# One expert layer in blocks of 512 slots instead of 256, handed to the next layer without a trip through memory

## The chip, the cores and the metric

The kernel runs on one core of a Trainium2 chip. The metric is the device time of one execution in microseconds (us); the median of three runs before the change is 4132.17 us. Engines are named as in the profile: PE (TensorE matmul), PEld (its weight loads), DVE (VectorE), ACT (ScalarE), POOL (GpSimd), SP (SyncE, which here only issues transfers).

## The reference

Three layers follow each other on 8 x 3072 = 24576 tokens of 256 features, all in 32-bit floats.

```
Y = rfft(x, axis=1) * (filt_r + 1j*filt_i);  x = irfft(Y)         # long convolution
e = argmax(x @ w_gate);  g = softmax(x @ w_gate)[e]                # one of 8 experts per token
x = g * (relu(x @ w1[e]) @ w2[e])                                  # 256 -> 1024 -> 256, "routed layer"
h = x @ w_in;  a = 0 if h <= -1, h if h >= 1, else (h+1)**2/4
out = a @ w_out                                                    # 256 -> 2048 -> 256, "dense layer"
```

## The kernel before, in words

**Convolution.** Some 650 us of transforms on all engines. For each of the 8 batches it also computes the gate, and ranks the tokens so that each expert's tokens can be found (`r_gate`, `r_cnt`, `r_rank`, `r_inv`, `r_out`). The ranking of the last two batches runs on while the routed layer has begun.

**Slots.** `slots` deals the tokens out to blocks; each block belongs to one expert. It runs twice: early, with the first 5 batches, for 16 full blocks, and late for the rest. `SURE` blocks are always computed; four more would be computed only if the last of the sure ones did not reach the last token (`rest`). The trace has 792 = 99 x 8 steps of blocks, so exactly the sure 99 ran.

**Routed layer.** A block j has 256 slots and eight steps f. Its tokens are gathered by POOL (`gather`: numbers first, then rows of 256 features), multiplied by the gate (`scale`, DVE), turned by PE (`take`) and split into a high and a low half, because every product is computed as three products of rounded halves. The expert's weights come in four loads of 512 KB (`load_w`, SP), and each step splits a part of them (`split_w`: ACT casts the high half `wh`, DVE or POOL subtracts the low half `wl`). Step f then has six matmuls in `b_in` (into a PSUM tile `h`), a Relu on ACT (`hh`), the low half on DVE (`hl`), and three steps later six matmuls in `b_out` into an accumulator `y1` which lasts for the block's eight steps. At the end of a block DVE copies `y1`, and SP stores it and the token numbers to memory (`s_y1T`, `s_idc`).

**Dense layer.** A chunk c has 512 tokens and sixteen steps. `load_c` reads it back from `s_y1T` and splits it. A step has six matmuls of 512 columns (`c_in`, into `h`), four elementwise instructions (DVE, ACT, DVE, ACT) and a subtraction on POOL, and three steps later twelve matmuls of 256 columns (`c_out`). Its four weight tables are loaded once in 16 transfers of 512 KB (`load_w2`).

**Order.** `run` writes the steps out by hand: first 14 blocks (112 steps, called the lead here), then for each chunk its 16 steps with 16 steps of blocks between them, while blocks last. `play` issues them; `plan` says how many steps ahead of use each load, cast and transpose stands. All engines run their instructions in this written order. The first 40-odd steps are dealt out one for one with the rest of the convolution's program, then two with each piece of the late `slots`; only after that does `dense` open the dense layer's buffers.

**PSUM.** Until `dense`, blocks have two banks for `h`, one tile `xt` for the transposes, one accumulator `y1`; `dense` adds a third `h` and a second `y1`.

Of the kernel before, what the change touches and what calls it, by code (L numbers as in the profile page):

```python
# [26 lines left out]
BLK = 256  # L27
NBLK = 103
EARLY = 5
SURE = 99  # L30
# [3 lines left out]
NE1 = 16  # L34
CH = 512
NCH = NTOK // CH

# [74 lines left out]

def slot_consts():
    c = np.zeros((128, 3 * NBLK + 16), np.float32)
    j = np.arange(NBLK)
    c[:, : 2 * NBLK] = (
        256 * j[None, :, None] + 128 * np.arange(2)[None, None, :] + np.arange(128)[:, None, None]
    ).reshape(128, -1)
    c[:, 2 * NBLK : 3 * NBLK] = j
    c[:8, 3 * NBLK : 3 * NBLK + 8] = np.eye(8)  # L120
    c[:, 3 * NBLK + 8 :] = np.arange(8)
    return c
# [492 lines left out]
def slots(tc, a, st, early, side=None):  # L615
# [4 lines left out]
    nb, j0, j1 = (EARLY, 0, NE1) if early else (NB, NE1, NBLK)  # L620
    J, K = j1 - j0, nb - 1
    per = 512 // J
    with ExitStack() as ctx:
# [4 lines left out]
        cst = p.tile([128, 3 * NBLK + 16], FP32, name="cst")  # L628
        nc.sync.dma_start(cst, a["c_b"])
        iota = cst[:, 0 : 2 * J].rearrange("p (j h) -> p j h", h=2)  # L630
        ij = cst[:, 2 * NBLK : 2 * NBLK + J]
        i8 = cst[:8, 3 * NBLK : 3 * NBLK + 8]
        ce = cst[:, 3 * NBLK + 8 : 3 * NBLK + 16]
# [15 lines left out]
        if early:  # L649
            V.tensor_copy(ti, cum[:, nb, :])  # L650
        else:
            V.tensor_tensor(out=tn, in0=cum[:, nb, :], in1=used, op=ALU.subtract)
            V.tensor_scalar(out=tf, in0=tn, scalar1=float(BLK - 1), scalar2=None, op0=ALU.add)
            V.tensor_copy(ti, tf)
            sums(cb, tn)
        V.tensor_scalar(out=ti, in0=ti, scalar1=8, scalar2=None, op0=ALU.logical_shift_right)
# [7 lines left out]
        V.tensor_scalar(out=Q[:, QO, :], in0=pb[:, 0:8], scalar1=-float(BLK), scalar2=None, op0=ALU.mult)  # L664
        yield
        if early:
            V.tensor_scalar(out=used, in0=pb[:, 0:8], scalar1=-1.0, scalar2=float(NE1), op0=ALU.mult, op1=ALU.add)
            V.scalar_tensor_tensor(out=used, in0=used, scalar=0.0, in1=tf, op0=ALU.max, op1=ALU.min)
            V.tensor_scalar(out=used, in0=used, scalar1=float(BLK), scalar2=None, op0=ALU.mult)
        else:  # L670
            V.tensor_tensor(out=Q[:, QC, :], in0=cb[:, 0:8], in1=Q[:, QO, :], op=ALU.add)
            V.tensor_tensor(out=Q[:, QO, :], in0=Q[:, QO, :], in1=used, op=ALU.add)
# [19 lines left out]
        pp = ctx.enter_context(tc.tile_pool(name="b_ps", bufs=1, space=PSUM, side=side))  # L692
        parts = [(k, min(k + per, NQ)) for k in range(0, NQ, per)]
        ps = []
        for i, (k0, k1) in enumerate(parts):
            ps.append(pp.tile([128, per, J], FP32, name=f"q{i}"))
            nc.tensor.matmul(ps[i][:, : k1 - k0], one[:8], QJ[:, k0:k1], start=True, stop=True)
        C = lambda k: ps[k // per][:, k % per]
        yield
        qs = p.tile([128, NQ, J], FP32, name="qs")  # L700
        for (k0, k1), v in zip(parts, ps):
            nc.scalar.copy(qs[:, k0:k1], v[:, : k1 - k0])
            if not early:
                yield
        ecf = p.tile([1, 2, J], FP32, name="ecf")
        V.tensor_copy(ecf[:, 0], C(QE)[:1])
        V.scalar_tensor_tensor(out=ecf[:, 1], in0=ij[:1], scalar=float(BLK), in1=C(QC)[:1], op0=ALU.mult, op1=ALU.add)
        V.tensor_scalar(
            out=ecf[:, 1], in0=ecf[:, 1], scalar1=float(BLK * j0), scalar2=float(NTOK), op0=ALU.add, op1=ALU.min
# [3 lines left out]
        r = p.tile([128, J, 2], FP32, name="r")  # L713
        x = p.tile([128, J, 2], FP32, name="x")
        KS = K if early else 1
        t = p.tile([128, KS, J, 2], FP32, name="t")
        B = lambda k: qs[:, k].unsqueeze(2).to_broadcast([128, J, 2])
        V.tensor_tensor(out=r, in0=iota, in1=B(QO), op=ALU.add)
        V.tensor_tensor(out=x, in0=r, in1=B(QB), op=ALU.add)
        for k in range(0, K, KS):  # L720
            n = min(KS, K - k)
            tk = t[:, :n]
            over = lambda k: qs[:, k : k + n].unsqueeze(3).to_broadcast([128, n, J, 2])
            V.tensor_tensor(out=tk, in0=r[:].unsqueeze(1).to_broadcast([128, n, J, 2]), in1=over(k), op=ALU.is_ge)
            V.tensor_tensor(out=tk, in0=tk, in1=over(K + k), op=ALU.mult)
            s = tk[:, 0]
            if n > 1:
                s = r
                V.tensor_reduce(out=s, in_=tk.rearrange("p k j h -> p j h k"), op=ALU.add, axis=AX.X)
            V.tensor_tensor(out=x, in0=x, in1=s, op=ALU.add)  # L730
            yield
        V.tensor_scalar(out=st["idx"][:, j0:j1], in0=x, scalar1=float(NTOK - 1), scalar2=None, op0=ALU.min)
# [3 lines left out]
class Ffn:  # L736

    LAG, LEAD, SKIP = 3, 26, (0, 6)  # L740

    def __init__(self, ctx, tc, a, st, nblk=NBLK, nch=NCH):
        self.nc, self.tc, self.a, self.st, self.nblk, self.nch = tc.nc, tc, a, st, nblk, nch
# [10 lines left out]
        self.nh = self.ny = 0  # L754
# [4 lines left out]
        self.E, self.RAW, self.W, self.ROW, self.X, self.H, self.CY, self.ACC, self.OUT = ({} for _ in range(9))  # L759

    def dense(self, ctx):
# [4 lines left out]
        self.gp = pool("c_g", 6)  # L766
        self.cyp, self.ap, self.op = (pool(n, 2, side="right") for n in ("c_cy", "c_a", "c_o"))
        self.ps_h.append(pool("cs_h2", 1, space=PSUM))
        self.ps_y.append(pool("cs_y2", 1, space=PSUM))
# [50 lines left out]
    def gather(self, j, more):  # L820
        nc = self.nc
        on = lambda ap: bass.IndirectOffsetOnAxis(ap=ap, axis=0)
        rows_of = lambda t: t[: S * EARLY] if j < NE1 else t
        if not more:
            ids = self.idp.tile([128, 2, 2], I32, name="ids")
            for h in range(2):
                nc.gpsimd.indirect_dma_start(
                    out=ids[:, h, :], out_offset=None, in_=rows_of(self.a["L"]),
                    in_offset=on(self.st["idx"][:, j, h : h + 1]),
                )  # L830
            self.ROW[j] = [ids]
            return
        ids = self.ROW[j][0]
        for h in range(2):
            r = self.rowp.tile([128, 256], FP32, name="row")
            nc.gpsimd.indirect_dma_start(out=r, out_offset=None, in_=rows_of(self.a["y"]), in_offset=on(ids[:, h, 0:1]))
            self.ROW[j].append(r)

    def scale(self, j):
        ids, *rows = self.ROW[j]  # L840
        for h in range(2):
            self.nc.vector.tensor_scalar(
                out=rows[h], in0=rows[h], scalar1=ids[:, h, 1:2].bitcast(FP32), scalar2=None, op0=ALU.mult
            )

    def take(self, j, i):
        nc = self.nc
        ids, *rows = self.ROW[j]
        ps = self.psx.tile([128, 2, 256], FP32, name="xt")
        for h in range(2):  # L850
            for k in range(2):
                nc.tensor.transpose(ps[:, k, 128 * h : 128 * h + 128], rows[h][:, 128 * k : 128 * k + 128], self.st["ident"])
        hi = self.xp.tile([128, 2, 256], F32R, name="xh")
        lo = self.xp.tile([128, 2, 256], F32R, name="xl")
        self.halves(i, ps[:], hi[:], lo[:], True)
        self.X[j] = (hi, lo)

    def b_in(self, j, f):
        nc = self.nc
        (xh, xl), (wh, wl) = self.X[j], self.W[j, f]  # L860
        o = self.h_tile()[:, :256]
        seq = [(w, x, k) for k in range(2) for w, x in ((wh, xh), (wh, xl), (wl, xh))]
        for n, (w, x, k) in enumerate(seq):
            nc.tensor.matmul(o, w[:, k, :], x[:, k, :], start=n == 0, stop=n == 5)  # L864
        hi = self.hp.tile([128, 256], F32R, name="hh")
        lo = self.hp.tile([128, 256], F32R, name="hl")
        nc.scalar.activation(hi, o, ACTF.Relu)  # L867
        yield
        nc.vector.scalar_tensor_tensor(out=lo, in0=o, scalar=0.0, in1=hi[:].bitcast(FP32), op0=ALU.max, op1=ALU.subtract)  # L869
        self.H[j, f] = (hi, lo)  # L870

    def b_out(self, j, f):
        nc = self.nc
        (hi, lo), (wh, wl) = self.H.pop((j, f)), self.W.pop((j, f))
        if f == 0:
            self.ny = (self.ny + 1) % len(self.ps_y)
            self.ACC["b"] = self.ps_y[self.ny].tile([128, 2, 256], FP32, name="y1")
        acc = self.ACC["b"]
        for d in range(2):
            for n, (w, x) in enumerate(((wh, hi), (wh, lo), (wl, hi))):  # L880
# [291 lines left out]
```

## Time and profile before

| | |
|---|---|
| median of 3 runs (range) | 4132.17 us (4128.89 to 4134.86) |
| the profiled execution | 4136.24 us, of which span of the profile 4134.3 us |
| PE busy | 3963.8 us (96%) |
| DVE, POOL, ACT busy | 63%, 63%, 53% |
| mean granted TensorE clock | 0.983 of full |

The span is the time from the first to the last instruction of the profiled execution; the 1.9 us around it belong to its time as well. A PE that is busy is not thereby at its peak: matmuls overlap, so what one costs is read from the distance between the starts of two, not from its duration.

### The profile page before, as it was taken

How to read it: one execution, taken by the hardware profiler on the slowest of the kernel's cores; microseconds unless marked ns; L12 is line 12 of the kernel's file. 1: busy time of each engine (PE TensorE's matmuls, PEld its weight loads, DVE VectorE, ACT ScalarE, POOL GpSimd, SP SyncE). 2: the span in 40 equal slices, each digit the busy share in tenths (PEclk: the TensorE clock that was granted, in tenths of full speed). 3: DMA queues.
4: the chain of work that ended last, by engine and by line, in shares of the span. 5: the costliest groups of instructions: out<-in, count | busy, mean ns of one | idle time of the engine just before them, and what ended most of it. 6: DMA issues, size and time to landing. Idle time of an engine off the chain costs nothing. (4 is left out here: it accounts for less than half of the span.)

```text
span 4134.3 us, 74872 instructions
## 1 busy us (share of the span) xinstructions
PE 3963.8 (96%) x27792; PEld 3556.8 (86%) x27792; DVE 2623.4 (63%) x4136; ACT 2198.3 (53%) x4246; POOL 2610.2 (63%) x2362
## 2 busy tenths in 40 slices
PE   8988888779999999999999999999999999999999
PEld 5665556779999999999999999999999999999988
DVE  5899996655665665656666656666566665666554
ACT  4765664445555555555555555555555555555544
POOL 5777775546666666666666666666666666666555
PEclk9999998889999999999999999999999999999999
DMA  9877766785455455544444554554445555544100
GB/s 294 259 223 216 224 188 154 147 178 132 93 92 92 92 93 93 92 89 92 92 93 93 93 93 93 92 93 93 93 92 93 93 93 92 90 91 92 37 22 16
DMA packets 327202, 473.28 MB, mean 114 GB/s; under 512 B 84304, under 2 KB 225008, under 8 KB 326832
## 3 DMA queue, kind: packets, MB, share of 16 engines
q1 hardware_dynamic: 293104, 408.61, 48.3%
q0 software_dynamic: 25056, 51.36, 3.9%
q10 hardware_dynamic: 8672, 8.48, 0.9%
q8 instruction: 220, 3.60, 0.4%
q14 instruction: 150, 1.23, 0.1%
HBM read 358.19 MB, written 110.14 MB: 113 GB/s over the span
## 5 line engine op out<-in xcount | busy, mean ns | idle before, releaser
L782 POOL TENSOR_TENSOR gl<-m,gh 128x512 fp32r<-128x512 f32 x768 | 1048.2, 1365 | 1085.4 <-ACT gh L919 603.9
L916 ACT ACTIVATE m<-m,half 128x512 f32<-128x512 f32 x768 | 556.0, 724 | 894.5 <-DVE m L915 841.0
L918 DVE SCALAR_TENSOR_TENSOR m<-h,m 128x512 f32<-128x512 f32 x768 | 531.0, 691 | 586.5 <-ACT m L916 538.3
L939 PE MATMUL o<-woh,gl 128*128 128x256 f32 x3084 | 875.0, 284 | 3.0 <-POOL gl L782 0.5
L939 PE MATMUL o<-woh,gh 128*128 128x256 f32 x3084 | 868.0, 281 | 3.0 <-ACT os L932 2.8
L939 PE MATMUL o<-wol,gh 128*128 128x256 f32 x3084 | 869.1, 282 | 0.0
L919 ACT CAST gh<-m 128x512 fp32r<-128x512 f32 x768 | 476.4, 620 | 588.2 <-DVE m L918 579.1
L915 DVE TENSOR_SCALAR m<-h 128x512 f32<-128x512 f32 x768 | 528.9, 689 | 299.7 <-PE h L911 219.4
L869 DVE SCALAR_TENSOR_TENSOR hl<-h,hh 128x256 fp32r<-128x256 f32 x792 | 333.6, 422 | 483.1 <-ACT hh L867 364.0
L911 PE MATMUL h<-cyh,winh 128*128 128x512 f32 x1536 | 607.6, 396 | 1.0 <-DVEq L1023 1.0
L911 PE MATMUL h<-cyh,winl 128*128 128x512 f32 x1536 | 603.9, 393 | 0.0
L911 PE MATMUL h<-cyl,winh 128*128 128x512 f32 x1536 | 602.5, 392 | 0.0
L939 PEld LDWEIGHTS o<-woh,gl 128*128 128x128 f32 x3084 | 586.2, 190 | 11.8 <-POOL gl L782 11.6
L939 PEld LDWEIGHTS o<-woh,gh 128*128 128x128 f32 x3084 | 586.3, 190 | 8.4 <-ACT os L932 4.5
L782 POOL TENSOR_TENSOR wl<-raw,wh 128x512 fp32r<-128x512 f32 x396 | 522.9, 1321 | 110.7 <-ACT wh L786 97.6
L939 PEld LDWEIGHTS o<-wol,gh 128*128 128x128 f32 x3084 | 584.4, 190 | 3.6
L786 ACT CAST wh<-raw 128x512 fp32r<-128x512 f32 x792 | 486.2, 614 | 106.5 <-DMA raw<-in_w_dram 68.8
L864 PE MATMUL h<-xh,wh 128*128 128x256 f32 x1584 | 456.7, 288 | 41.2 <-DVE hl L869 32.0
L881 PE MATMUL y<-hh,wh 128*128 128x256 f32 x1584 | 457.4, 289 | 7.8 <-DVE y1s L887 7.7
L864 PE MATMUL h<-xl,wh 128*128 128x256 f32 x1584 | 452.6, 286 | 1.1 <-issue 0.8
L881 PE MATMUL y<-hh,wl 128*128 128x256 f32 x1584 | 451.5, 285 | 2.1 <-issue 2.1
L881 PE MATMUL y<-hl,wh 128*128 128x256 f32 x1584 | 449.8, 284 | 0.1
(185 smaller groups left out, 7708.1 us busy)
## 6 DMA issues: line engine op xcount, KB each, us to landing
raw<-in_w_dram SPq DMA_DIRECT2D x396, 512.0 KB
f<-in_filt_dram SPq DMA_DIRECT2D x72, 384.0 KB
s_y1T<-y1s SPq DMA_DIRECT2D x99, 256.0 KB
xt<-in_x_dram SPq DMA_DIRECT2D x64, 384.0 KB
s_z<-zs SPq DMA_DIRECT2D x128, 192.0 KB
zt<-s_z SPq DMA_DIRECT2D x64, 384.0 KB
s_y<-y SPq DMA_DIRECT2D x128, 192.0 KB
cy<-s_y1T SPq DMA_DIRECT2D x48, 512.0 KB
```

The costliest lines, as they stand in the source:

```text
L782: eng.tensor_tensor(out=lo, in0=src, in1=hi.bitcast(FP32), op=ALU.subtract)
L786: self.at(i, lambda: self.nc.scalar.copy(hi, src))
L864: nc.tensor.matmul(o, w[:, k, :], x[:, k, :], start=n == 0, stop=n == 5)
L869: nc.vector.scalar_tensor_tensor(out=lo, in0=o, scalar=0.0, in1=hi[:].bitcast(FP32), op0=ALU.max, op1=ALU.subtract)
L881: nc.tensor.matmul(acc[:, d, :], w[:, 2 + d, :], x, start=(f == 0 and d == 0 and n == 0), stop=(f == 7 and n == 2), skip_group_check=True,)
L911: nc.tensor.matmul(ps, w[:, k, 128 * f : 128 * f + 128], x[:, k, :], start=n == 0, stop=n == 5)
L915: V.tensor_scalar(out=m, in0=ps, scalar1=-1.0, scalar2=1.0, op0=ALU.max, op1=ALU.min)
L916: nc.scalar.activation(m, m, ACTF.Square, bias=self.half[:, 0:1], scale=-0.5)
L918: V.scalar_tensor_tensor(out=m, in0=ps, scalar=-1.0, in1=m, op0=ALU.max, op1=ALU.add)
L919: nc.scalar.copy(hi, m)
L939: self.nc.tensor.matmul(self.ACC["c"][t // 2][:, t % 2, :], x[:, 128 * t : 128 * t + 128], w[:, f, :], start=(f == 0 and t % 2 == 0 and n ...
```

## The change

The 99 blocks of 256 slots become 41 blocks of 512 slots (all full) and 17 sure blocks of 256 for what is left over (four more in reserve, as before). 41 x 2 + 17 = 99, so the number of slots is the same. A wide step has the same twelve matmuls, on 512 columns. At the end of a wide block, `b_end` splits `y1` itself, two ACT copies and two DVE subtractions, straight from PSUM into the tiles that the dense chunk reads. For blocks 6 to 40 that is all: chunk j is block j. Blocks 0 to 5 and the narrow ones are stored, in halves, and read back by `load_c` later. The lead has 60 wide steps in place of 112 narrow ones. Chunks go in the order 6 to 40, 0 to 5, 41 to 47; each takes 8 wide steps along, and from the third on every other chunk takes a whole narrow block along as well. `slots` runs three times, and `dense` is called before the two late ones. PSUM: `y1` now takes two banks and there is only one of it; before `dense`, `take` borrows an `h` tile. The pools of weight tiles, raw weights, `hh`/`hl` and dense activations each lose one or two buffers, and `split_w` stands 3 (lead) or 6 (later) steps ahead of use instead of 5 or 7, `load_w` 7 or 14 instead of 9 or 17.

```
-BLK = 256
-NBLK = 103
-SURE = 99
+CH = 512
+NW = 41
+NS = 21
+NBLK = NW + NS
+SURE = NBLK - 4
+LEADERS = 6
...
-        self.rawp, self.wp = pool("c_raw", 4), pool("c_w", 9)
-        self.idp, self.rowp = pool("c_id", 8), pool("c_row", 4)
-        self.xp, self.hp, self.y1p = pool("c_x", 2), pool("c_h", 5), pool("c_y1", 2)
-        self.ps_h, self.ps_y = [pool("cs_h", 2, space=PSUM)] * 2, [pool("cs_y", 1, space=PSUM)]
-        self.psx = pool("cs_x", 1, space=PSUM)
+        self.rawp, self.wp = pool("c_raw", 3), pool("c_w", 7)
+        self.idp, self.idl, self.rowp = pool("c_id", 12), pool("c_il", LEADERS), pool("c_row", 8)
+        self.xp, self.hp, self.y1p, self.cyp = pool("c_x", 2), pool("c_h", 4), pool("c_y1", 1), pool("c_cy", 2)
+        self.ps_h, self.ps_y = [pool("cs_h", 2, space=PSUM)] * 2, pool("cs_y", 1, space=PSUM)
+        self.psx = None
...
+        ps = self.psx.tile([128, CH], FP32, name="xt") if self.psx else self.h_tile()
...
         if f == 7:
-            s = self.y1p.tile([128, 2, 256], FP32, name="y1s")
-            nc.vector.tensor_copy(s, acc)
-            c = nc.sync.value_load(self.st["ec"][0:1, 1, j : j + 1], min_val=0, max_val=NTOK)
-            nc.sync.dma_start(self.a["y1T"][:, :, bass.ds(c, BLK)], s)
-            ids = self.ROW.pop(j)[0]
-            nc.sync.dma_start(self.a["idc"][bass.ds(c, BLK)].rearrange("(h p) o -> p (h o)", p=128), ids[:, :, 0])
+            self.b_end(j, acc, n)
+
+    def b_end(self, j, acc, n):
+
+        nc, a = self.nc, self.a
+        pool = self.cyp if j < NW else self.y1p
+        hi, lo = (pool.tile([128, 2, n], F32R, name=x) for x in ("cyh", "cyl"))
+        for k in range(2):
+            nc.scalar.copy(hi[:, k], acc[:, k])
+            nc.vector.tensor_tensor(out=lo[:, k], in0=acc[:, k], in1=hi[:, k].bitcast(FP32), op=ALU.subtract)
+        if LEADERS <= j < NW:
+            self.CY[j] = (hi, lo, self.rows(self.IDS.pop(j)))
+            return
...
+        chunks = [*range(LEADERS, NW), *range(LEADERS), *range(NW, self.nch)]
+        wide = [("b", j, f) for j in range(NW) for f in range(8)]
+        narrow = [[("b", j, f) for f in range(8)] for j in range(NW, sure)]
+        lead = 8 * LEADERS + 12
+        steps, wide = wide[:lead], wide[lead:]
+        for m, c in enumerate(chunks):
+            more, wide = wide[:8], wide[8:]
+            if m >= 2 and m % 2 == 0 and narrow:
+                more[4:4] = narrow.pop(0)
+            n = max(8, len(more))
             for f in range(16):
-                steps += [("c", c, f), *more[f : f + 1]]
+                steps += [("c", c, f), *more[f * n // 16 : (f + 1) * n // 16]]
```

On PE, a step of the lead stands like this before (first half of `b_in` of one step, and the first of `b_out` of the step three earlier; `r` is the ranking of the convolution's last batches):

```order
L864 MATMUL h_7693<-xh_7434,wh_7478 128x256
L864 MATMUL h_7693<-xl_7435,wh_7478 128x256
L864 MATMUL h_7693<-xh_7434,wl_7479 128x256
...
L881 MATMUL y1_7439<-hh_7582,wh_7309 128x256
L881 MATMUL y1_7439<-hl_7583,wh_7309 128x256
L881 MATMUL y1_7439<-hh_7582,wl_7310 128x256
```

and like this after, with the transposes of the next block's tokens (`row`) where a step has them:

```order
L870 MATMUL h_7656<-xh_7345,wh_7519 128x512
L870 MATMUL h_7656<-xl_7346,wh_7519 128x512
L870 MATMUL h_7656<-xh_7345,wl_7520 128x512
...
L858 MATMUL h_7672<-ident_58,row_7318 128x128
L858 MATMUL h_7672<-ident_58,row_7320 128x128
L858 MATMUL h_7672<-ident_58,row_7322 128x128
L858 MATMUL h_7672<-ident_58,row_7324 128x128
L885 MATMUL y1_7480<-hh_7549,wh_7394 128x512
L885 MATMUL y1_7480<-hl_7550,wh_7394 128x512
L885 MATMUL y1_7480<-hh_7549,wl_7395 128x512
```

The number of matmuls in a step is the same and each has twice the columns; the transposes now write one of the two tiles `h`.

On SP, between two loads of weights (`raw`) in the lead, there stand before the store of one block (`s_y1T`, 256 KB) and of its token numbers:

```order
L809 DMA raw_7963<-in_w_dram 128x1024
L888 TENSOR_LOAD ec_62
L888 ISA x2
L889 REGISTER_ALU
L889 DMA s_y1T<-y1s_7974 256x1x256
L891 REGISTER_ALU
L891 DMA s_idc<-ids_7100 128x2x1
L809 ISA
L809 DMA raw_8035<-in_w_dram 128x1024
```

and after, for blocks 0 to 5 alone, the two halves of a wide block:

```order
L813 DMA raw_8032<-in_w_dram 128x1024
L911 DMA s_y1h<-cyh_8041 256x1x512
L911 DMA s_y1l<-cyl_8042 256x1x512
L813 ISA
L813 DMA raw_8096<-in_w_dram 128x1024
```

There are still four loads of weights between two such stores, but each pair of loads now feeds four wide steps.

## Rows read from the trace of the kernel before

**Rows 1.** The page: span, busy time by engine, the span in 40 slices.

```profile
span 4134.3 us, 74872 instructions
PE 3963.8 (96%) x27792; PEld 3556.8 (86%) x27792; DVE 2623.4 (63%) x4136; ACT 2198.3 (53%) x4246; POOL 2610.2 (63%) x2362
PE   8988888779999999999999999999999999999999
PEclk9999998889999999999999999999999999999999
DMA  9877766785455455544444554554445555544100
```

**Rows 2.** Windows: length, busy us (instructions) by engine, granted clock, DMA share, GB/s.

```profile
core 0: us, PE busy (x) PEld busy (x) DVE busy (x) ACT busy (x) POOL busy (x), PEclk, DMA share, GB/s
...
658.70:916.10 257.40, 209.04 (x1543) 194.47 (x1540) 174.64 (x344) 119.91 (x268) 139.03 (x117) 0.90 0.81 163
916.10:994.10 78.00, 70.21 (x484) 65.39 (x483) 39.79 (x67) 36.19 (x68) 37.89 (x32) 0.96 0.66 152
994.10:1063.30 69.20, 69.14 (x491) 64.69 (x490) 42.42 (x68) 36.71 (x70) 44.24 (x40) 1.00 0.54 92
1063.30:3834.00 2770.70, 2764.69 (x19523) 2585.84 (x19522) 1677.95 (x2681) 1468.20 (x2761) 1766.72 (x1598) 1.00 0.50 92
...
3889.10:3935.30 46.20, 45.50 (x290) 40.96 (x289) 24.53 (x35) 23.07 (x36) 25.55 (x25) 1.00 0.16 46
```

**Rows 3.** PE's timeline in the dense stage: start, us, instruction; one group's first each.

```profile
2002.05 0.39 PE L911 MATMUL h<-cyh,winh 128*128 128x512 f32 x1
...
2003.44 0.28 PE L881 MATMUL y<-hh,wh 128*128 128x256 f32 x1
...
2004.87 0.28 PE L939 MATMUL o<-woh,gh 128*128 128x256 f32 x1
```

**Rows 4.** Waits in window 658:916, of PE, ACT and SP: total us, times, longest.

```profile
PE h L864 <- DVE hl L869: 32.0, 17, 4.0
PE y L881 <- DVE y1s L887: 7.7, 7, 2.2
...
ACT wh L786 <- DMA raw<-in_w_dram: 51.2, 16, 6.6
...
SPq L889 <- DVE hl L869: 24.8, 5, 7.0
```

**Rows 5.** Timelines of ACT, DVE and PE, one wait in the lead.

```profile
890.15 0.62 ACT L786 CAST wh<-raw 128x512 fp32r<-128x512 f32 x1 [6.45 <-DMA raw<-in_w_dram]
890.68 0.38 ACT L867 ACTIVATE hh<-h 128x256 fp32r<-128x256 f32 x1
...
891.09 0.42 DVE L869 SCALAR_TENSOR_TENSOR hl<-h,hh 128x256 fp32r<-128x256 f32 x1 [5.12 <-ACT hh L867]
...
891.57 0.39 PE L864 MATMUL h<-xh,wh 128*128 128x256 f32 x1 [2.82 <-DVE hl L869]
```

**Rows 6.** The page's groups: weights' cast and low half, and their loads.

```profile
L786 ACT CAST wh<-raw 128x512 fp32r<-128x512 f32 x792 | 486.2, 614 | 106.5 <-DMA raw<-in_w_dram 68.8
...
raw<-in_w_dram SPq DMA_DIRECT2D x396, 512.0 KB
```

**Rows 7.** Tile xt: cast and subtraction of 512 columns from PSUM, ns min/median/max.

```profile
L786 ACT CAST xh<-xt x99: 576/579/597, 658.0 to 3830.8; 128x512 fp32r<-128x512 f32 x99
L782 DVE TENSOR_TENSOR xl<-xt,xh x99: 674/680/684, 658.8 to 3833.5; 128x512 fp32r<-128x512 f32 x99
```

**Rows 8.** PE's wait in window 994:4134, at the start of a chunk's outputs.

```profile
PE o L939 <- ACT os L932: 2.8, 4, 0.7
```

More of the change, by code (lines that the diff above doesn't have):

```diff
@@ L691, in slots @@
         yield
[L692 to L698, printed above, removed]
-        yield
[L700 to L704, printed above, removed]
+        qs = p.tile([128, NQ, J], FP32, name="qs")
+        pp = pp or ctx.enter_context(tc.tile_pool(name="b_ps", bufs=1, space=PSUM, side=side))
+        ps = pp.tile([128, CH], FP32, name="xt")[:, : NQ * J].rearrange("p (q j) -> p q j", j=J)
+        nc.tensor.matmul(ps, one[:8], QJ, start=True, stop=True)
+        nc.scalar.copy(qs, ps)
+        yield
         ecf = p.tile([1, 2, J], FP32, name="ecf")
-        V.tensor_copy(ecf[:, 0], C(QE)[:1])
-        V.scalar_tensor_tensor(out=ecf[:, 1], in0=ij[:1], scalar=float(BLK), in1=C(QC)[:1], op0=ALU.mult, op1=ALU.add)
+        V.tensor_copy(ecf[:, 0], qs[:1, QE])
+        V.scalar_tensor_tensor(out=ecf[:, 1], in0=ij[:1], scalar=float(W), in1=qs[:1, QC], op0=ALU.mult, op1=ALU.add)
         V.tensor_scalar(
-            out=ecf[:, 1], in0=ecf[:, 1], scalar1=float(BLK * j0), scalar2=float(NTOK), op0=ALU.add, op1=ALU.min
+            out=ecf[:, 1], in0=ecf[:, 1], scalar1=float(CH * (j0 if whole else NW)), scalar2=float(NTOK),
+            op0=ALU.add, op1=ALU.min,
         )
@@ new lines, in rows, with load_c @@
+    def rows(self, ids):
+        return [ids[:, t, 0:1] for t in range(4)]
+    def load_c(self, c):
+        nc = self.nc
+        hi, lo = (self.cyp.tile([128, 2, CH], F32R, name=x) for x in ("cyh", "cyl"))
+        for y, t in (("y1h", hi), ("y1l", lo)):
+            nc.sync.dma_start(t[:].bitcast(FP32), self.a[y][:, :, CH * c : CH * c + CH])
+        if c < NW:
+            ic = self.rows(self.IDS.pop(c))
+        else:
+            ic = self.idp.tile([128, 4], I32, name="ic")
+            nc.sync.dma_start(ic, self.a["idc"][CH * c : CH * c + CH].rearrange("(t p) o -> p (t o)", p=128))
+            ic = [ic[:, t : t + 1] for t in range(4)]
@@ L981, in run @@
     def run(self):
-        first = 14
         self.now = -self.LEAD
-        sure = min(SURE, self.nblk)
-        steps = [("b", j, f) for j in range(first) for f in range(8)]
-        for c in range(self.nch):
-            j = first + 2 * c
-            more = [("b", j, f) for j in range(j, min(j + 2, sure)) for f in range(8)]
+        sure = SURE
+        chunks = [*range(LEADERS, NW), *range(LEADERS), *range(NW, self.nch)]
[8 more added lines that the diff above has]
+            n = max(8, len(more))
             for f in range(16):
-                steps += [("c", c, f), *more[f : f + 1]]
+                steps += [("c", c, f), *more[f * n // 16 : (f + 1) * n // 16]]
+        assert not wide and not narrow
         pos = {x: i for i, x in enumerate(steps)}
@@ L1107, in tile_fftconv_moe_moe @@
                         i = next(blocks)
-        for _ in slots(tc, a, st, False):
-            next(blocks)
-            next(blocks)
         ffn.dense(end)
+        for k in (1, 2):
+            for _ in slots(tc, a, st, k, ffn.psx):
+                next(blocks)
         for _ in blocks:
```

232 lines of the change are left out of this document (114 added, 118 removed).

## The prediction

> **What bounds the kernel now.** Start with the page [rows 1]. PE is busy 96% of the span and no other engine above 63%. So an engine that gets less to do gains nothing by itself; what counts is how long PE takes for its work, and where it stands still or runs slowly. The slices show where that is: from the eleventh slice on, PE is full and its clock is at 1.0; before that there are 8s among the 9s, and the clock has 8s in slices 7 to 9. The changed code begins in slice 7.
>
> The windows put numbers on it [rows 2]. I cut at the first routed step (658.7), the first dense step (916.1), one and two chunks on (994.1, 1063.3), and where the blocks run out (3834). From 1063 to 3834 PE is idle 2770.7 - 2764.7 = 6 us: there only cheaper PE work can help. In the lead, 658.7 to 916.1, it is idle 257.4 - 209.0 = 48.4 us. The clock there is 0.90 on average, and its levels are 1.2 and 2.4 GHz, so 20% of the lead, 51 us, ran at half speed; with PE busy 81% of the time, about 21 us of that busy time would not be there at full clock. The first chunk takes 78.0 us where the next takes 69.2.
>
> What makes PE stand still in the lead is in the waits [rows 4] and one of them step by step [rows 5]. PE's longest entry is the low half `hl` of a step's hidden values, 32.0 us, then the copy of the accumulator, 7.7 us in 7 waits. The timeline shows what is behind `hl`: ACT sat 6.45 us for a load of weights, cast it, and only then came to the Relu `hh` that stood behind it in its order; DVE had waited 5.12 us for that Relu, and PE 2.82 us for DVE. Those loads cost ACT 51.2 us of waiting. They are late for two reasons: a narrow step lasts 12 matmuls, and every second one needs 512 KB (the 396 loads of [rows 6]), and SP, which issues them, stands at stores of finished blocks in between (24.8 us in 5 waits for one store's cause alone). The transfer engines are 0.81 busy there against 0.50 later [rows 2].
>
> **The wide step.** In the dense stage PE never waits, so distances between starts are prices [rows 3]. Six matmuls of 512 columns take 2003.44 - 2002.05 = 1.39 us, or 232 ns each. The next twelve, the 256-column matmuls of a block step, take 2004.87 - 2003.44 = 1.43 us, or 119 ns each. A wide step is twelve of the first kind, 2.78 us; the two narrow steps it replaces take 2.86 us. It saves 0.08 us, and there are 41 x 8 = 328 of them: 26 us. Of these 268 stand outside the lead: 21.4 us. The bounds are nothing, if `b_out`, which never ran with 512 columns, should be worse by as much as `b_in` is better, and 26 us.
>
> The Trainium skill, "TensorE: Matmul & The Clock Gate", section "Back-to-back issue gap", gives an isolated matmul its columns at full clock and 2.5 ns on top, which would make the 3936 matmuls saved worth some 10 us, an estimate from that page. The trace does not agree: its distances leave about 6 ns per matmul saved, so the sum goes by the rows.
>
> **The lead.** Now: 257.4 us for 112 narrow steps. Those are 112 x 1.43 = 160 us; 48 us are idle and 21 us slow clock; the remaining 28 us are PE work of the ranking, transposes and the late slots, which stays. After: 60 x 2.78 = 167 us, the same 28 us, and idle and slow time of which I must choose the size. One end is 69 us, as now. The other is 8 us, the accumulator's waits of today alone. For the low end speaks that the cause of most waits is halved: a load of 512 KB now feeds two wide steps, 5.6 us in place of 2.9 us, and it is issued 7 steps ahead of its place, 19.5 us, where 9 narrow steps were 12.9 us. ACT has in a step one Relu of 512 columns and one weight cast, about 0.58 + 0.61 us [rows 6, 7], in 2.78 us, where it had 0.38 + 0.61 us in 1.43.
>
> What speaks for more than the low end is PSUM. While `take` holds one of the two `h` tiles, `b_in` of each step writes the other, and must wait until Relu and `hl` of the step before have read it. Priced by [rows 7] that is 0.58 + 0.68 us and hand-overs of under 0.1 us, as [rows 5] have them between ACT, DVE and PE (a Relu ends at 891.06, `hl` starts at 891.09, ends at 891.51, and PE starts at 891.57): about 1.4 us, beside the 1.39 us of `b_out` that PE does meanwhile. So it is hidden by a hair, and whatever DVE or ACT does for the ranking in between shows up. At a block's end the accumulator must be emptied before the next `b_out`: two casts on ACT and the last subtraction, 0.58 + 0.58 + 0.68 = 1.9 us against 1.39 us of `b_in`, some 0.5 to 1.5 us for each of 7 ends; and the two casts hold up the next Relu. I take 10 us for the ends, 12 us for collisions with the ranking in the first 41 steps and 8 us of slow clock: 30 us in place of 69. The lead then takes 167 + 28 + 30 = 225 us, 32 us less, and holds 120 narrow steps' worth in place of 112, which saves another 8 x 1.43 = 11.4 us later.
>
> **The dense stage.** Blocks 6 to 40 are no longer stored and read back, their weights are split once for 512 slots, and DVE, ACT and POOL all get lighter. On PE that is worth nothing, since it waited 6 us in 2770. The cover for the things that got tighter there: at a block's end 1.9 us of emptying lies beside at least one step's `c_out`, one `b_in` and one `c_in` half, 1.43 + 2 x 1.39 = 4.2 us where wide and narrow blocks meet, more elsewhere. If it failed, each of 35 wide ends and 17 narrow ones would pay what exceeds 4.2 us. The first chunk's excess of 8.8 us is due to the same weight loads beside the dense tables; with half the former I give back 4 us. Chunks without blocks have a wait of 0.7 us each at the start of their outputs [rows 2, 8], which block steps hide elsewhere. Wide steps run out after 268/8 = 33.5 chunks and the last narrow block stands in the 35th, so 13 chunks are bare in place of 5: +5.6 us. The first gather takes four lists of numbers and rows instead of two before the first step can start; POOL is not full, and I add 2 us (0 to 6).
>
> **Sum.** -32 -11.4 -21.4 -4 +5.6 +2 = -61 us, from the profiled execution's 4136.2 us (span 4134.3 and 1.9 around it; 4 us above the median): 4075 us.
>
> **Rivals.**
> *Lead unchanged.* The ranking and not the weights sets the lead's pace, or the borrowed `h` tile gives back what the loads gave: idle and slow time stay at 69 us. For it: DVE is busy 68% of the lead, and the ranking's instructions stand between its `hl`. Against it: ACT's waits are for loads. 4075 + 39 = 4114 us.
> *Only columns count.* Wide steps save nothing: 4075 + 26 = 4101 us.
> *Lead near the limit.* Idle and slow time fall to 8 us: 4075 - 22 = 4053 us.
> *Slower: one accumulator.* In every block end the four instructions of `b_end` come late, because ACT and DVE have other work queued ahead of them, and PE stands before the next `b_out`. Today the lead's single accumulator costs 1.1 us per end with one instruction in the chain [rows 4]. With 58 ends, 61 us of gain and 8 us of threshold are used up at 1.2 us of wait each on average; at one dense step, 2.8 us, it would be 4075 + 162 = 4237 us. The Trainium skill, "Perfetto Trace Analysis", section "Matmuls" under "Optimizing Tensor Performance", wants independent groups of matmuls to rotate through PSUM banks, so that one is emptied while the next is filled; this change drops a rotation. No dense row of before can show it, since two accumulators were there; what speaks against it is the 4.2 us of cover.
> *The change doesn't do what it says*, because more than 17 narrow blocks are needed and `rest` runs: 11.4 us for each. From the reference's inputs the experts get 2715, 3307, 3367, 3037, 2826, 3511, 3318 and 2495 tokens; what 41 full blocks leave fills 17 narrow ones, so I give it nothing.
>
> **How the numbers follow.** The forecast, gains in the lead and in the step, gets 0.60. Lead unchanged 0.16, only columns 0.04, near the limit 0.10, the accumulator 0.06, and 0.04 for gains and waits that cancel. A measurement tells about 0.2%, 8 us, from no change. Faster is the first four, 0.90; same 0.04; slower 0.06. The range takes in all but the last two cases and the forecast's own bounds: idle and slow time between 10 and 69 us, which is 4055 to 4114, and 8 us more below for the first chunk and the bare chunks: 4046 to 4114.
>
> **What would show it.** Between the first dense step and the end of the blocks, starts of `b_in` and `b_out` matmuls 232 ns apart; there, no more than 10 us of waits for `cyl`. The first dense step at about 886 us after 60 wide steps, the granted clock of the lead above 0.95, and ACT's wait for `raw` below 15 us. Wrong would be a lead that PE spends waiting for `hl` with weights already there, a dense stage in which PE waits at every eighth block step, or a span that is shorter by the lead alone.

## The result, and the profile after

| | before | after |
|---|---|---|
| median (range), 4 runs each | 4130.53 us (4127.86 to 4134.86) | 4177.2 us (4170.94 to 4179.17) |
| ratio to before, 95% interval | | 1.0109 (1.0092 to 1.0127) |
| profiled execution | 4136.24 us | 4179.17 us |
| first routed step, first dense step | 658.7, 916.1 us | 658.1, 884.3 us |
| PE idle in the lead, in the dense stage (to PE's last matmul) | 48.4, 17.8 us | 27.1, 107.8 us |

The change makes the kernel slower by 1.1%; the forecast was 4075 us and faster. The lead came out as forecast to within 2 us. The dense stage lost all of it and more.

The page of after, as in [rows 1]: span, PE's busy time, then PE, granted clock and DMA in 40 slices.

```profile
span 4177.4 us, 63452 instructions
PE 3937.2 (94%) x23852; PEld 3345.2 (80%) x23852; DVE 2280.7 (55%) x3643; ACT 2020.2 (48%) x3625; POOL 2334.2 (56%) x2202
...
PE   8988887899999999999999999999999999999999
...
PEclk9999988999999999999999999999999999999999
DMA  9877764341211211111212111111121121111110
```

PE does 27 us less, DVE 343 and POOL 276 us less, transfers fall from 5 to 1 or 2 tenths, and the span is 43 us longer. PE is still the busiest engine; what is new is that it stands still for longer. The slices hide it, since 9 means anything from 90%. The windows show where; they stand against [rows 2]:

```profile
core 0: us, PE busy (x) PEld busy (x) DVE busy (x) ACT busy (x) POOL busy (x), PEclk, DMA share, GB/s
658.10:884.30 226.20, 199.12 (x915) 149.98 (x910) 138.58 (x270) 95.68 (x174) 98.81 (x93) 0.95 0.42 136
...
957.10:1026.90 69.80, 68.25 (x393) 59.58 (x392) 33.97 (x53) 32.77 (x54) 35.22 (x34) 1.00 0.13 42
1026.90:1113.40 86.50, 82.25 (x499) 73.08 (x498) 41.41 (x72) 39.45 (x72) 48.35 (x48) 0.98 0.23 72
957.10:3598.00 2640.90, 2545.55 (x15071) 2241.57 (x15070) 1283.49 (x2100) 1225.85 (x2133) 1421.01 (x1349) 0.99 0.19 59
```

The first row is the lead. The next two are one chunk with a wide block beside it (69.8 us, PE idle 1.5) and one with a wide and a narrow block (86.5 us, idle 4.2). Over the stretch with blocks PE is idle 2640.9 - 2545.6 = 95 us, where it was 6 us in 2771 before, and the granted clock is 0.99 where it was 1.00. What ends those waits, for PE from 884 us on, as in [rows 8]:

```profile
PE xt L858 <- DVE xl L786: 78.7, 50, 2.8
PE y L885 <- DVE cyl L899: 18.8, 16, 1.2
PE o L964 <- ACT os L957: 7.9, 11, 0.7
```

Two new waits, 97.5 us together. The timeline shows one of each. First the end of a wide block before a narrow one (around 1058 us), then the second half of a block's transposes (around 1082 us):

```profile
1057.47 0.40 PE L885 MATMUL y<-hh,wh 128*128 128x512 f32 x1
...
1058.62 0.39 PE L885 MATMUL y<-hh,wl 128*128 128x512 f32 x1
1058.85 0.28 PE L870 MATMUL h<-xh,wh 128*128 128x256 f32 x1
...
1060.47 0.62 ACT L790 CAST wh<-raw 128x512 fp32r<-128x512 f32 x1
...
1060.99 0.58 ACT L898 CAST cyh<-y 128x512 fp32r<-128x512 f32 x1
...
1061.60 0.69 DVE L899 TENSOR_TENSOR cyl<-y,cyh 128x512 fp32r<-128x512 f32 x1 [1.69 <-ACT cyh L898]
...
1062.33 0.59 ACT L898 CAST cyh<-y 128x512 fp32r<-128x512 f32 x1 [0.76 <-DVE cyl L899]
...
1062.95 0.69 DVE L899 TENSOR_TENSOR cyl<-y,cyh 128x512 fp32r<-128x512 f32 x1 [0.65 <-ACT cyh L898]
...
1063.70 0.39 PE L885 MATMUL y<-hh,wh 128*128 128x256 f32 x1 [1.18 <-DVE cyl L899]
...
1080.09 0.58 ACT L790 CAST xh<-xt 128x512 fp32r<-128x512 f32 x1
...
1080.56 0.62 ACT L790 CAST wh<-raw 128x512 fp32r<-128x512 f32 x1
...
1081.09 0.38 ACT L872 ACTIVATE hh<-h 128x256 fp32r<-128x256 f32 x1
1081.50 0.42 DVE L874 SCALAR_TENSOR_TENSOR hl<-h,hh 128x256 fp32r<-128x256 f32 x1 [1.98 <-ACT hh L872]
...
1081.84 0.68 DVE L940 TENSOR_SCALAR m<-h 128x512 f32<-128x512 f32 x1
1082.44 0.68 DVE L786 TENSOR_TENSOR xl<-xt,xh 128x512 fp32r<-128x512 f32 x1
...
1083.27 0.61 PE L858 MATMUL xt<-ident,row 128*128 128x128 f32 x2 [1.89 <-DVE xl L786]
```

**The transposes.** `xt` is one bank of PSUM. Before, one `take` filled it once per block, and the next came a block later. Now every block, wide or narrow, fills it twice, three steps apart, and the second filling must wait until `xl` has read the first. `xl` could start at 1080.67, when `xh` is done. But DVE works in written order, and `hl` and the dense step's `m` stand ahead of it; `hl` waits for a Relu that stands behind `xh` and `wh` on ACT. So `xl` ends at 1083.12, and PE has stood since 1081.38.

**The accumulator.** Its last matmul ends at 1059.01. ACT comes to the first cast 2 us later, after the dense step's square, `gh` and `wh`. Then the four instructions run one after the other, 1060.99 to 1063.64, since each waits for the one before.

### The profile page after: what moved, and what is told of

It reads as the page before. It is cut to its first block, busy times and chain, and to the rows that moved or that the text cites. A ratio compares the mean times of both kernels' runs of the same rounds, so it can differ in the third digit from the quotient of the medians.

```text
span 4177.4 us, 63452 instructions
## 1 busy us (share of the span) xinstructions
PE 3937.2 (94%) x23852; PEld 3345.2 (80%) x23852; DVE 2280.7 (55%) x3643; ACT 2020.2 (48%) x3625; POOL 2334.2 (56%) x2202
## 5 line engine op out<-in xcount | busy, mean ns | idle before, releaser
L786 POOL TENSOR_TENSOR gl<-m,gh 128x512 fp32r<-128x512 f32 x768 | 997.6, 1299 | 1407.8 <-ACT gh L944 883.2
L964 PE MATMUL o<-woh,gh 128*128 128x256 f32 x3084 | 879.5, 285 | 8.1 <-ACT os L957 7.9
L874 DVE SCALAR_TENSOR_TENSOR hl<-h,hh 128x512 fp32r<-128x512 f32 (+1 forms) x464 | 284.2, 612 | 661.1 <-ACT hh L872 659.8
L964 PEld LDWEIGHTS o<-woh,gh 128*128 128x128 f32 x3084 | 586.8, 190 | 38.8 <-ACT os L957 12.6
L964 PEld LDWEIGHTS o<-wol,gh 128*128 128x128 f32 x3084 | 588.3, 191 | 27.1 <-DMA wol<-s_w2s 1.5
L885 PE MATMUL y<-hh,wh 128*128 128x512 f32 (+1 forms) x928 | 343.4, 370 | 21.4 <-DVE cyl L899 21.4
L786 POOL TENSOR_TENSOR wl<-raw,wh 128x512 fp32r<-128x512 f32 x232 | 303.7, 1310 | 96.0 <-ACT wh L790 85.0
L870 PE MATMUL h<-xh,wh 128*128 128x512 f32 (+1 forms) x928 | 341.7, 368 | 5.1 <-DVE hl L874 4.1
L936 PEld LDWEIGHTS h<-cyh,winl 128*128 128x128 f32 x1536 | 289.1, 188 | 67.8
L870 PE MATMUL h<-xh,wl 128*128 128x512 f32 (+1 forms) x928 | 338.2, 364 | 5.1 <-POOL wl L786 4.6
L870 PE MATMUL h<-xl,wh 128*128 128x512 f32 (+1 forms) x928 | 337.6, 364 | 0.0
L885 PE MATMUL y<-hh,wl 128*128 128x512 f32 (+1 forms) x928 | 337.2, 363 | 0.0
```

The lines of the kernel that those rows point to most:

```text
L786: eng.tensor_tensor(out=lo, in0=src, in1=hi.bitcast(FP32), op=ALU.subtract)
L870: nc.tensor.matmul(o, w[:, k, :], x[:, k, :], start=i == 0, stop=i == 5)
L885: nc.tensor.matmul(acc[:, d, :], w[:, 2 + d, :], x, start=(f == 0 and i == 0), stop=(f == 7 and i == 2), skip_group_check=True,)
L936: nc.tensor.matmul(ps, w[:, k, 128 * f : 128 * f + 128], x[:, k, :], start=n == 0, stop=n == 5)
L964: self.nc.tensor.matmul(self.ACC["c"][t // 2][:, t % 2, :], x[:, 128 * t : 128 * t + 128], w[:, f, :], start=(f == 0 and t % 2 == 0 and n ...
```

## The experiments

Ratios are against the kernel before, run beside the experiment on its chip; its medians there were 4125.89 us (for the first four experiments), 4128.29 (the repeat of after, the two on the kernel before, and the earlier multiplication), 4126.72 (the second bank, and the later gathers on top of other edits) and 4120.25 us (the last two). The code cuts show the lines that matter, with ... where lines are left out.

**Takes four steps apart**, `gap` being 4 in the dense stage and still 3 in the lead.

```
-                self.plan(p, j, ahead=6, lead=8)
+                self.plan(p, j, ahead=6, lead=8, gap=4)
...
-            at(i - 7 + 3 * k, lambda k=k: self.take(j, k, i - 6 + 3 * k))
+            t = i - 4 - gap + gap * k
+            at(t, lambda k=k, t=t: self.take(j, k, t + 1))
```

> The changed kernel, with the first of a block's two takes one step earlier wherever the dense layer runs too; nothing else. Theory A (order): PE's 78.7 us of waits for xt come from DVE's order: the subtraction xl that frees xt after the first take stands behind m of the same step, and m waits for that step's matmuls, after which PE at once wants xt again. One step more between the takes puts xl ahead of that m: the waits fall below 5 us, most of the twelve stretches of slow clock of 3.4 us in the dense stage go with them (some 20 us), and the time is 4080 to 4100 us. Theory B (bank): one bank that is filled twice per block must make PE wait whatever the order: waits stay at 70 to 80 us and the time at 4170 to 4180 us.

4120.59 us, ratio 0.9986 (0.9976 to 0.9996): 20 us above the range expected. PE's waits in the dense stage:

```profile
PE y L885 <- DVE cyl L899: 18.8, 16, 1.2
PE xt L858 <- DVE row L847: 11.0, 21, 1.1
...
PE xt L858 <- DVE xl L786: 0.5, 1, 0.5
```

One step of distance takes 78.7 us to 0.5. The wait on `cyl` stays. A small new one comes: the first take now stands a step earlier and sometimes meets the gate's multiplication (`row`), which was not moved. The stretches at 1.2 GHz that the trace records in the dense stage, 37.5 us together in after, are gone. The new wait and a first dense step at 895.6 us, where after had 884.3, are about what is missing to the range; that later start is taken up below.

**The low half ahead of the dense step's `m`.** Distance as in after; `play` issues a pending split before a step's own elementwise work.

```
-                next(g)
             go(self.fill, i)
+            next(g, None)
```

> The changed kernel, with the split's subtractions (xl, wl) of a step issued ahead of the step's own first elementwise instruction; the takes stay where they are. Theory A (order): xl no longer stands behind m, so PE's waits for xt fall below 10 us and the time is 4080 to 4105 us, with up to 10 us more than the run with the gap, where xl and wl, put first, delay m. Theory B (bank): no change, 4170 to 4180 us.

4153.14 us, ratio 1.0063 (1.0046 to 1.008): a far smaller gain than expected. PE's wait is still there, at half its size:

```profile
PE xt L858 <- DVE xl L786: 42.3, 34, 2.2
```

and DVE's timeline before one of them shows why:

```profile
1085.99 0.42 DVE L874 SCALAR_TENSOR_TENSOR hl<-h,hh 128x256 fp32r<-128x256 f32 x1 [1.97 <-ACT hh L872]
1086.33 0.68 DVE L786 TENSOR_TENSOR xl<-xt,xh 128x512 fp32r<-128x512 f32 x1
```

`m` is out of the way, but `xl` still stands behind the `hl` of the step before, and that behind ACT. In after the waits are of three sorts, 16 each of 1.2, 1.5 and 1.9 us; here the first is gone, the second is down to 0.3 and the third is 2.0. So the place on DVE is one part of the cause, and this timeline puts the other on the queue on ACT; I had named only the first. The clock did not gain: the dense stage has 54.6 us at 1.2 GHz here.

**An accumulator of two tiles.** Same two banks, one tile each.

```
-            self.ACC["b"] = self.ps_y.tile([128, 2, CH], FP32, name="y1")
+            self.ACC["b"] = [self.ps_y.tile([128, CH], FP32, name=f"y1{d}") for d in range(2)]
...
```

> The changed kernel, with the accumulator y1 as two tiles of one bank each instead of one tile of two banks, so that each half is released by its own cast and subtraction. PE waits 18.8 us for cyl, 16 times 1.2 us where a narrow block follows a wide one: the four instructions run one after the other (2.7 us) and start 2 us late behind gh and wh on ACT. If that is the whole price of the single accumulator (A and B alike), the wait falls below 4 us and the time to 4155 to 4165 us. If the accumulator is the main loss (theory C), the time falls below 4130 us.

4146.76 us, ratio 1.005 (1.0033 to 1.0066). No wait of PE for `cyl` is left, and the one on `xl` stays at 78.0 us. The time is 8 us below the range expected. The clock has a part in that: only 3.4 us at 1.2 GHz are left in the dense stage. The timeline of the same block end as above:

```profile
1058.85 1.07 ACT L898 CAST cyh<-y 128x512 fp32r<-128x512 f32 x2
1059.46 1.29 DVE L899 TENSOR_TENSOR cyl<-y,cyh 128x512 fp32r<-128x512 f32 x2 [1.69 <-ACT cyh L898]
```

The two casts now follow each other and the subtractions overlap them: 1.90 us from the first to the last, which is the chain that I had forecast, against 2.65 us with one tile. Where `y1` is one tile, the program has the second cast wait for DVE's first subtraction, though that reads the other half; with two tiles it waits for PE alone.

**Both of these edits.**

> Both edits: the first take one step earlier and the accumulator as two tiles. Theory A: the gains add, since they are waits of PE at different places: 4060 to 4085 us, under 30 us of idle PE after the first dense step. Theory B: only the accumulator's, 4155 to 4165 us.

4096.13 us, ratio 0.9923 (0.9907 to 0.994), 11 us above the range expected. With these two waits gone the change gains. The largest wait left is the multiplication, 19.3 us in 29 waits.

**Both, and the multiplication two steps earlier.**

```
...
-        at(i - 9, lambda: self.scale(j))
+        at(i - 6 - gap - (gap > 3), lambda: self.scale(j))
```

> The changed kernel with both edits that gained (first take one step earlier, accumulator as two tiles), and the multiplication by the gate two steps earlier: with the first take earlier, PE waited 19.3 us, 29 times, for that multiplication (DVE row). Theory A: it is the same kind of wait, an instruction of DVE that stands too close to the transposes in the written order; with two steps more it goes below 3 us, and the time to 4072 to 4085 us. If DVE is simply too full there, the waits move to another instruction and the time stays at 4090 to 4100 us.

4078.03 us, ratio 0.9876 (0.986 to 0.9893). No wait for a take is left in the dense stage. The time lies 3 us from the forecast's 4075, but partly by chance: the two stalls that the forecast had not seen are out, the lead takes 212.6 us and not 225, the first routed step comes at 669.7 us, where the first profile of after had 658.1, and PE has a new wait of 12.6 us (15 times) for `gl`, the low half that POOL makes in a dense step.

**The changed kernel once more**, to compare with on the same chip.

> The changed kernel as it is, once more, on the chip of the next three runs. In the four runs so far the first block step stood at 670 to 674 us of the span, against 658 in the profile of the changed kernel, though the program up to there is the same but for a few buffers. If that belongs to the chip or the execution, it shows here as well, with a time of 4165 to 4185 us; if it came with the edits, the first block step is at 658 us here.

4190.06 us, ratio 1.0149 (1.0132 to 1.0166). The dense stage repeats (78.9 us on `xl`, 18.8 on `cyl`, 41 us at 1.2 GHz). New is the first routed step: at 671.2 us, where the first profile of after had 658.1. So it does not come with the edits: it changes from one run of the same kernel to another.

**The kernel before, with the turn alone in two halves.** Blocks of 256, but each block fills `xt` twice, three steps apart; as in after, the multiplication moves two steps ahead with it. The rest is as before.

```
...
-        at(i - 7, lambda: self.scale(j))
-        at(i - 4, lambda: self.take(j, i - 3))
+        at(i - 9, lambda: self.scale(j))
+        for k in range(2):
+            at(i - 7 + 3 * k, lambda k=k: self.take(j, k, i - 6 + 3 * k))
```

> The kernel before with one part of the change alone: the turn of a block's tokens in two takes three steps apart, each through the one tile xt, as in the changed kernel (half the columns each). Theory A (order): the second take finds xl behind m of a dense step, and PE waits about 0.7 us for m, 0.4 for xl and the hand-overs, 1.2 to 1.6 us in each of 85 blocks: 100 to 135 us more, 4225 to 4260 us. Rival: the wait needs the changed kernel's mix of steps or its 512 columns; then 4125 to 4145 us.

4340.79 us, ratio 1.0515 (1.0497 to 1.0533). More than expected. This one edit, without wide steps, a single accumulator or direct chunks, makes the same wait, once for nearly every block:

```profile
PE xt L853 <- DVE xl L782: 145.9, 84, 3.6
```

That is 1.7 us each, as in after (1.6). The span is 206 us longer, and three parts make 203 of it: this wait; 11 us up to the first dense step; and half of the 92 us more that the dense stage spends at 1.2 GHz (99 us, before 7).

**The kernel before, with one accumulator** instead of two in the dense stage.

```
-        self.ps_y.append(pool("cs_y2", 1, space=PSUM))
```

> The kernel before with a single accumulator y1 in the dense stage too. Rival (an accumulator that doesn't rotate costs at each block end what it cost in the lead, 1.1 us, or more): 85 ends, 4220 us and above. Theory: what counts is the chain at the end against the work in between; here it is one copy of 0.7 us that stands up to 2 us late behind m on DVE, beside 3.5 us of other matmuls, so under 5 us of waits for y1s and 4125 to 4140 us.

4128.45 us, ratio 1.0003 (0.9994 to 1.0013). From the first dense step (908.5 us) on PE never waits for it; the last such wait, 3.7 us at 900 us, is in the lead, where the kernel before has one accumulator too. So there, with one instruction to empty it, a single accumulator costs nothing that can be measured; in after, with four serial instructions, it does.

**A second bank for the transposes** in place of the third `h`; takes three steps apart, as in after.

```
-        self.ps_h.append(pool("cs_h2", 1, space=PSUM))
-        self.psx = pool("cs_x", 1, space=PSUM)
+        self.psx = pool("cs_x", 2, space=PSUM)
```

> The changed kernel with two PSUM banks for the transposes xt in the dense stage, for which the third tile h is given up; order and everything else as in the changed kernel. The theory that xt is one bank filled twice three steps apart, and that its second filling stands behind an xl that DVE reaches late: the second filling goes to the other bank and waits for nothing, so the 79 to 82 us of waits on xl go to under 3 us, though xl itself is as late as before; by that alone 4177 to 4190 less 79 and less about 13 of slow clock, 4085 to 4098 us. A rival in which xl's lateness itself is what PE pays for (its next block cannot start): the wait moves to b_in's xl with about the same 80 us. The third h is missed on top: each h is held from c_in's or b_in's end until its last reader on DVE, some 1.4 to 2 us, beside about 2.8 us of other work on PE; by that it costs little, but with DVE behind by the same m and xl I expect 10 to 60 us of waits for h, and 4095 to 4150 us in all.

4095.21 us, ratio 0.992 (0.9903 to 0.9936). PE waits for no `xl` any more, with the order on DVE unchanged. The missing `h` costs 4.8 us, less than the 10 to 60 expected:

```profile
PE y L884 <- DVE cyl L898: 20.1, 17, 1.4
...
PE h L935 <- DVE m L942: 4.8, 10, 0.5
```

**Later gathers.** This is for the start. In the repeat of after, POOL issued 24 gathers in a row, 1.25 us apart, from 628 us on, and a small instruction of the ranking stood behind 16 of them:

```profile
647.62 0.94 POOL L833 DMA_INDIRECT idl<-s_L,idx  x1 [0.30 <-issue]
648.55 0.14 POOL L408 MEMSET cnt<- 128x8 f32 x1
...
664.21 0.71 DVE L414 TENSOR_TENSOR_SCAN t<-keep,cnt 128x264 f32<-128x264 bf16 x1 [18.46 <-ACT cnt L410]
```

The queue does not delay the start every time. In the first profile of after the memset stood behind 16 gathers too and came even later, but the scan followed 1.5 us behind it:

```profile
650.58 0.13 POOL L408 MEMSET cnt<- 128x8 f32 x1
...
652.12 0.76 DVE L414 TENSOR_TENSOR_SCAN t<-keep,cnt 128x264 f32<-128x264 bf16 x1
```

The edit lets blocks 1 to 7 gather numbers and rows 16 and 12 steps ahead, not 26 and 17, on top of the 4078 us version.

```
-        at(p[0] - 26, lambda: self.gather(j, False))
-        at(p[0] - 17, lambda: self.gather(j, True))
+        late = 1 <= j <= LEADERS + 1
+        at(p[0] - (16 if late else 26), lambda: self.gather(j, False))
+        at(p[0] - (12 if late else 17), lambda: self.gather(j, True))
```

> The version with one accumulator bank per half, takes four steps apart and the scaling earlier (4078.0 us), with one more edit: blocks 1 to 7 gather their token numbers 16 steps ahead of use instead of 26 and their rows 12 instead of 17, so that 4 and not 12 lists of numbers stand on POOL before the first block's rows. Theory A (POOL's order): the first block step comes at 670 us instead of 658 because 28 gathers of 1.25 us stand in a row on POOL from 630 us on, and the ranking's small POOL instruction (the memset of cnt, seen at 648.6 and 650.0 us, with DVE's scan waiting 17.5 to 18.5 us in the chain behind it) stands behind 16 of them. Then the memset comes before 641 us, the scan's wait falls below 6 us, the first block step comes at 655 to 661 us, and the time is 13 us shorter: 4065 us (4060 to 4070). Theory B (the delay is due to something else, such as memory or the order of transfers on SP): first step still at 668 to 675 us, time within 4 us of 4078. Against both: rows that come too late for the scaling in the lead would show as waits of DVE's row for its load and cost up to 10 us.

4057.43 us, ratio 0.9828 (0.9812 to 0.9845). The memset comes at 641.4, the first routed step at 656.4 in place of 669.7, and the lead takes 204.4 us in place of 212.6. The scan's wait fell to 6.4 us only, a little above the bound I had set.

**After, with the later gathers alone.**

> The changed kernel with the later gathers of blocks 1 to 7 alone. If POOL's queue of gathers is a cost of its own, the first block step comes at 655 to 661 us in place of 671.2 us, the lead takes some 213 us in place of 221.5 us, and the waits on xl (about 80 us) and cyl (about 20 us) in the dense stage stay: from 4177 to 4190 us it goes to 4154 to 4168 us, still slower than the kernel before. If the start only moves idle time into the lead, the first dense step stays at 890 to 893 us and the time within 5 us of 4185.

4163.84 us, ratio 1.0103 (1.0087 to 1.012): first routed step at 651.5, lead 216.3 us, dense waits unchanged (79.0 and 18.7 us). Against the repeat of after, the start is a cost of its own, and the smaller one. The memset and the scan of this run:

```profile
641.01 0.17 POOL L408 MEMSET cnt<- 128x8 f32 x1
...
645.47 0.70 DVE L414 TENSOR_TENSOR_SCAN t<-keep,cnt 128x264 f32<-128x264 bf16 x1
```

**Two banks for `xt`, two tiles for `y1`, later gathers.**

> The changed kernel with two banks for xt (the third h given up), one bank for each half of y1, and the later gathers of blocks 1 to 7; the takes stay three steps apart and nothing else moves. If the three stalls are independent and banks do the same as order, the sum of the single prices holds: 4095.2 us (two banks for xt alone) less 20 us (cyl) less 15 us (start) less 8 us (lead) = 4052 us (4045 to 4058); dense waits on xl and cyl under 3 us, on h about 5 us, first block step 655 to 661 us. If the missing third h costs more once the other waits are gone, the waits for h rise above 15 us and the time is above 4060 us.

4032.57 us, ratio 0.979 (0.9773 to 0.9806), the fastest of all and 20 us better than the sum of the single prices. The 4.8 us for `h` are gone too, and PE is idle 11.2 us in the whole dense stage. Its windows of two chunks, as those of after above:

```profile
920.40:988.50 68.10, 68.10 (x394) 59.67 (x393) 33.89 (x54) 32.47 (x54) 35.40 (x34) 1.00 0.14 44
988.50:1069.20 80.70, 80.69 (x500) 71.87 (x499) 41.28 (x72) 39.03 (x72) 48.49 (x48) 1.00 0.25 76
```

PE is full, and the chunks take 68.1 and 80.7 us. 9 of the 20 us are a first routed step at 647.5 us against the 656.4 of the run before with later gathers, and some 8 are a shorter lead (203.2 us); why these stages vary so was not tried.

## Why the prediction was wrong, step by step

**The wide step** was right. Six matmuls of 512 columns take 1058.85 - 1057.47 = 1.38 us in `b_out` too, so the lower bound (a worse `b_out`) did not come. With the stalls gone a chunk with a wide block takes 68.1 us: the 46.1 us of a bare chunk and 8 x 2.78 = 22.2 make 68.3.

**The lead** was right in its sum: 226.2 us against 225, first dense step at 884.3 against 886, granted clock 0.95, and no wait of ACT for `raw` among the leading ones, where it was 51.2 us. The make-up was a little different: idle time and the clock's loss make some 38 us (27.1 us idle and half of the 24 us at 1.2 GHz) where I took 30, and the ranking and late slots 21 where I took 28. The largest cause of idle time is the borrowed `h` tile that `take` fills and that waits for `xl` (9.3 us in 4 waits); I had looked for the ranking there. That was the dense stage's stall in small, in a place where I had priced `take`.

**"The cover for the things that got tighter there"** is the step that failed. I listed one thing that got tighter in the dense stage, the emptying of the accumulator. The second was in the change (`plan` and `take`): transposes in two halves into one bank. I priced a cast and a subtraction of `xt` [rows 7] by their durations and asked what PE does meanwhile in the lead, but for the dense stage I never asked who fills `xt` again, and when. Two instructions of 1.3 us together in three steps of time looked harmless; what counts is when ACT and DVE come to them. That cost 78.7 us. The run on the kernel before shows it alone, and the distance of four steps and the second bank each remove it. I had named the sign, a PE that waits at every eighth block step of the dense stage: it came, 50 times, nearly once per block.

**The accumulator's 4.2 us of cover** was wrong by two terms. Where a wide block meets a narrow one, the `b_in` beside it is narrow, 0.70 us and not 1.39, so the cover is 1062.52 - 1059.01 = 3.5 us (the wait's start less the last matmul's end). The chain is 2.65 us and not 1.9, and starts 2 us late. So it fails before 16 of 17 narrow blocks by 1.2 us, and at no other end of the dense stage. The rival "one accumulator" had the mechanism, with ACT's queue, but put it at every end; the measured size is 18.8 us, not the 69 from which it would have decided. The Trainium skill, "Perfetto Trace Analysis", section "Matmuls", the rule on rotating banks, is borne out for `xt`: with a second bank PE's 79 us of waits were gone. For the accumulator it made no difference in the kernel before (ratio 1.0003); in after the single one costs 18.8 us of waits, and a second one was not tried there.

**The clock.** I gave the dense stage none of it. The trace records 37.5 us there at 1.2 GHz (11 stretches of 3.4 us), against 6.8 before; at half speed that is some 15 us of lost work. In the four runs without the waits on `xl` and `cyl` it is 0 to 3.4 us. But it does not follow from each stall. With four steps of distance, where the waits on `cyl` are left, it is 0; with two accumulator tiles, where 78.0 us of waits on `xl` are left, it is 3.4 us. After one wait of 1.9 us on `xl` each, in after (where a wait on `cyl` had come before it) and with two tiles (where none had), the granted clock (third figure from the end) of the next 3.4 us is:

```profile
core 0: us, PE busy (x) PEld busy (x) DVE busy (x) ACT busy (x) POOL busy (x), PEclk, DMA share, GB/s
1083.30:1086.70 3.40, 3.40 (x17) 3.40 (x18) 1.04 (x2) 1.14 (x2) 2.77 (x4) 0.51 0.05 1
...
1080.00:1083.40 3.40, 3.40 (x29) 3.40 (x30) 1.50 (x3) 1.91 (x5) 2.77 (x4) 1.00 0.04 1
```

In after 10 of 16 such waits have a slow stretch behind them, with two tiles none of 16. So in these kernels it took both kinds of wait, and taking out either gives nearly all of the 15 us back. In the kernel before with turns in two halves, waits on `xl` were enough alone; why there is open.

**First chunk, bare chunks, first step.** The first chunk took 72.8 us, 5.2 less than before (I gave 4; 1.1 of the 5.2 is the cheaper wide steps, 69.2 - 68.1). Bare chunks take 46.1 us, 13 of them, as counted. The first step's 2 us were 0 in the first profile and 11 to 15 in seven other profiled executions with these gathers; I bounded them at 6, since POOL is not full. It is not full on average, but for 30 us it is; in the first profile too, though, so that alone does not make the start late.

**The sum.** 4075 us + 79 + 19 (waits) + 15 (clock) = 4188 us, against 4179.2 for the profiled execution; the sum of the other terms was thus 9 us too high. The failure lies in two waits, both on instructions that are short and stand in the wrong place.

**What stays open.** The later gathers move the first step: in the three runs with them it came at 647.5 to 656.4 us, in the eight runs of wide blocks without them at 658.1 to 673.6. The links in between are not: in the repeat of after the scan starts 16 us after the memset, in the first profile of after 1.5, and PE's and ACT's waits there are put down to "issue" and "remote", for which the profile names no releaser of this program.

## What to carry to other kernels

When a change makes a buffer turn over more often, ask of every buffer, not of the largest: who reads it last, what stands ahead of that reader on its engine, and which step's data that waits for. Cover is the time from the reader's turn to the next write, not the reader's duration against the work in between. Waits of 1 to 2 us that come once per block are invisible in the slices, moved PE's share only from 96% to 94%, and were worth 2% here; the cheapest cures were one step more of distance, or a bank taken from a buffer that could spare it.

## What was not expected of the hardware

Gaps of 1 to 4 us brought the granted clock down in some kernels and not in others: 99 us at 1.2 GHz in the dense stage of the kernel before with turns in two halves, 37.5 us in after, but 3.4 us with two accumulator tiles, with 50 gaps of 1 to 2 us left. The slow stretches added some 46 us to 146 us of waits in the first and 15 to 97 in the second. And gathers cost POOL 1.25 us apiece whatever they bring: lists of numbers (8 bytes a row) and rows of 1 KB were issued at the same pace.
